# Summing the two sides of the model axis in PSUM in the first batch's cosine DFT

## The chip, the cores and the metric

The kernel runs on one core of a Trainium2 chip. The metric is the device time of one execution in microseconds, as the median of several runs. Engine names in the profile: PE is TensorE (PEld its weight loads), DVE is VectorE, ACT is ScalarE, POOL is GpSimd, SP is SyncE, whose queue issues the loads and stores here.

## What is computed

Four batches of 768 tokens, 8 heads of 64. Retention (a recurrent linear attention) comes first, then a Fourier mix over tokens and model axis, and a normalised two-layer network:

```python
for t in range(S):                                   # S = 768
    state = gamma * state + einsum('bhd,bhe->bhde', k[:, :, t], v[:, :, t])
    y[:, :, t] = scale * einsum('bhd,bhde->bhe', q[:, :, t], state)
x = y.transpose(0, 2, 1, 3).reshape(B, S, H * D)     # B = 4, H * D = 512
mixed = real(fft(fft(x, axis=1), axis=2))
u = x + mixed
un = (u - mean(u)) / sqrt(var(u) + 1e-6)
out = u + maximum(un @ w_ch1, 0) @ w_ch2             # 512 -> 2048 -> 512
```

## The kernel before

**Retention** is done in six chunks of 128 tokens, for a pair of heads at a time: transposes of q and k (tq), scores masked into atm, states by a scan (s), and the outputs wkY, which ScalarE writes as f16 into x (x0_unit in the first batch). Pair 3 is the last pair done; it fills columns 130 to 257 of side 1.

**The layout of x** serves the folds. A row of 512 channels lies as two sides: side 0 has channels 0 to 255 in order, side 1 the upper ones mirrored, so that a column holds channel d of side 0 and its mirror image of side 1. `fold_s` (L673) adds and subtracts the two halves of the token axis into xab, `fold_d` (L683) adds (e = 0, for the cosine) and subtracts (e = 1, for the sine) the two sides into eo, in two blocks of 128 columns (cb = 0, 1).

**The DFT** has two stages. Stage one, `s1_unit(b, e, cb)`, multiplies eo by tables over the token axis (csp for the cosine, ssp for the sine): six matmuls with 193 columns into one PSUM buffer, two parities of three token blocks each. A copy brings the result to g as f16, in group gi = 2e + cb. In the first batch ScalarE copies groups 0 and 1 (L737) and VectorE groups 2 and 3 (L739). Stage two, `s2_unit`, multiplies g by tables over the model axis (cd16, sd16) for one block kb of 128 tokens of the result, copies the sine part to qn (L855) and adds up u (L856, L858). `g0_unit` works out the one column that the tables leave out, and with `xmean_unit` and `mean_unit` the mean of each row, for the first three blocks of the first batch. `px_unit` adds x itself in PSUM there.

**The network.** `norm_unit` makes un, `unT_unit` transposes it (on TensorE for the first batch and for blocks 0 to 2 of the second, by DMA later), `h_unit` and `h0_unit` are the first layer, with an eviction on ScalarE for the fb in `ACT_ROWS` and on VectorE for the others, `ch_unit` the second layer, whose result is added to u and stored.

**What sets the order.** In the first batch `first_units` is a list, and `pin()` after each unit makes every engine keep the order in which the list issues instructions:

```python
    for u in first_units():
        u()
        pin()
```

`filler(n)` are n matmuls of 512 columns whose result nobody reads. From h0 on, `emit` sorts the units of all streams by due times: the products of a batch are spread evenly from b to b + 1, and the attention, the stages of the DFT and the transposes of the next batch get stretches of their own (`ts`, `da`, `dm`). A planner then sets the order of each engine by priority and readiness, starting from that order; the trace follows the due times closely but not in every place.

PSUM has a pool ps_g of five buffers for most of this, ps_y of two for wkY and px, and ps_pm of three for the network later. SyncE's loads of batch 1 wait for the last matmul of h0 for block 1 and for the weights.

Of the kernel before, what the change touches and what calls it, by code (L numbers as in the profile page):

```python
# [18 lines left out]
P = 128  # L19
# [11 lines left out]
ON_ACT = {'q': (0, 1, 0), 'kv': (1, 1, 1), 'g': (0, 1, 1), 'gr': (0, 0, 0)}  # L31
FB = 1
NPE = 2
ACT_ROWS = ((2, 4, 5, 6, 7, 8, 9, 10, 14), (0, 3, 6, 7, 9, 10, 11, 12, 14, 15), (2, 4, 5, 6, 7, 8, 9, 10, 14))


@with_exitstack
def kernel(
# [432 lines left out]
    def kv0_unit(i):  # L471
        def run():
            st = at[0, i]
            kd, v16 = kd_of[0, i], v16_of[0, i]
            wkf = st["wkf"] = ps_g.tile([P, D * (NCH - 1)], f32, tag="g", name="wkK",
                                        padded_shape=[P, DM])
            wk = wkf.rearrange("p (e c) -> p e c", c=NCH - 1)
            for c in range(NCH - 1):
                for h2 in range(2):
                    nc.tensor.matmul(wk[64 * h2:64 * h2 + 64, :, c], kd[:, c, h2, :],  # L480
                                     v16[:, c, h2, :], start=True, stop=True)
        return run
# [240 lines left out]
    def s1_unit(b, e, cb):  # L723
        def run():
            eo, g, gr = fd[b]["eo"], fd[b]["g"], fd[b]["gr"]
            tab = csp if e == 0 else ssp
            ps = ps_g.tile([P, 2, NK], f32, tag="g", name="ps1", padded_shape=[P, 2, 256])
            for par in range(2):
                for sb in range(3):
                    nc.tensor.matmul(ps[:, par, :],  # L730
                                     fd[b]["ee"][:, 2 * e + cb, par, sb, :] if b >= FB else
                                     eo[:, e, par, sb, 128 * cb:128 * cb + 128],
                                     tab[:, par, sb, :], start=(sb == 0), stop=(sb == 2))
            gi = 2 * e + cb
            dst = g[:, gi].rearrange("p (i t) -> p t i", t=2)
            if e == 0 or ON_ACT["g"][min(b, 2)]:
                nc.scalar.copy(dst, ps)  # L737
            else:
                nc.vector.tensor_copy(dst, ps)  # L739
            if b:  # L740
                (nc.scalar.copy if ON_ACT["gr"][min(b, 2)] else nc.vector.tensor_copy)(
                    gr[:, gi], g[:, gi, 384:0:-1])
        return run

    def gr_unit(gi):
# [285 lines left out]
    def first_units():  # L1031
        def a(i):
            un = [am_unit(i, 0), am_unit(i, 1)]
            return un

        def e(i, *hh):
            return [ae_unit(i, half, h2) for half, h2 in hh]

        def y(i):
            return [yi_unit(i, 0), yi_unit(i, 1)]  # L1040

        def x(i):
            return [x0_unit(i, 0), x0_unit(i, 1)]

        std = ((0, 0), (0, 1), (1, 0), (1, 1))
        heads = ((0, 0), (1, 0), (0, 1), (1, 1))
        o = PAIR_ORDER
        un = [ts_dve(0), gk_unit(o[0]), gk_unit(o[1]), t_act(0, 0), t_act(0, 1),
              q0_unit(0), t0_unit(0, 0), filler(4), ts_dve(1), te_unit(0, 0), t_act(0, 2),
              k0_unit(0), t0_unit(0, 1), filler(3), te_unit(0, 1), ts_dve(2), td_dve(0), t_act(1, 0),  # L1050
              t_act(1, 1), t_act(1, 2), v0_unit(0)]
        un += a(0) + [filler(1), kv0_unit(0)] + e(0, *std) + [sc_unit(0)]
        un += [q0_unit(1), t0_unit(1, 0), te_unit(1, 0), t_act(2, 0), t_act(2, 1), filler(4),
               k0_unit(1), t0_unit(1, 1), te_unit(1, 1)]
        un += y(0) + [parity_consts, yx_unit(0), filler(2)] + x(0) + [t_act(2, 2), v0_unit(1),
                                                                     half_ids]
        un += a(1) + [csn_unit(0), filler(1), kv0_unit(1)] + e(1, *std) + [sc_unit(1)]
        un += [q0_unit(2), t0_unit(2, 0), te_unit(2, 0), csn_unit(1), filler(3), k0_unit(2),
               t0_unit(2, 1), te_unit(2, 1)]
        un += y(1) + [td_dve(1), yx_unit(1), filler(2)] + x(1) + [  # L1060
            gk_unit(o[2]), t_act(3, 0), t_act(3, 1), v0_unit(2)]
        un += a(2) + [filler(1), kv0_unit(2)] + e(2, *std) + [sc_unit(2), t_act(3, 2),
                                                              csn_unit(2)]
        un += [q0_unit(3), w1_unit(0), t0_unit(3, 0), te_unit(3, 0), filler(3)] + y(2)
        un += [fold_s(0, 0, 258, 0, 1), g0_unit(0, (0,)), k0_unit(3), t0_unit(3, 1),
               te_unit(3, 1), yx_unit(2), gk_unit(o[3]), x0_unit(2, 0), x0_unit(2, 1),
               t_act(4, 0), t_act(4, 1), filler(2), v0_unit(3)]
        un += [w1_unit(g) for g in range(1, 4)] + [w2_unit(g) for g in range(4)]
        un += a(3) + e(3, (0, 0), (1, 0)) + [kv0_unit(3), filler(4), sc_unit(3), t_act(4, 2)]
        un += e(3, (0, 1), (1, 1))  # L1070
        un += [yx_unit(3), yi_unit(3, 0), x0_unit(3, 0), filler(1), yi_unit(3, 1), x0_unit(3, 1),
               g0_unit(0, (1,)), filler(1)]
        un += [fold_s(0, 0, 130, 1, 2), fold_d(0, 0), s1_unit(0, 0, 0), fold_s(0, 130, 258, 1, 2),
               px_unit(0), fold_d(0, 1, (0,)), xmean_unit(0), fold_d(0, 1, (1,)),
               s1_unit(0, 1, 0), s1_unit(0, 0, 1), s1_unit(0, 1, 1), g0_unit(0, (2,)),
               mean_unit(0)]
        un += [s2_unit(0, 0), px_unit(1), s2_unit(0, 1), norm_unit(0, 0), gr_unit(0), gr_unit(1),
               px_unit(2), filler(2), unT_unit(0, 0), xmean_unit(1), mean_unit(1),
               norm_unit(0, 1), s2_unit(0, 2), xmean_unit(2), mean_unit(2), norm_unit(0, 2),
               gr_unit(2), gr_unit(3), edge_zeros, x_edges(1)]  # L1080
        return un
# [25 lines left out]
    for b in range(B):  # L1107
        majors = []
        if b == 0:
            for kb in range(3):  # L1110
                if kb:
                    majors.append(unT_unit(0, kb))
                majors += [h0_unit(kb, g) for g in range(4)]
        else:
            majors += [h_unit(b, 0, fb) for fb in range(NFB)]
        majors.append(rstd_unit(b, 0))
        majors += [ch_unit(b, 0, rb3, part) for rb3 in range(3) for part in range(4)]
        majors += [h_unit(b, 1, fb) for fb in range(NFB)]
        majors.append(rstd_unit(b, 1))
        majors += [ch_unit(b, 1, rb3, part) for rb3 in range(3) for part in range(4)]  # L1120
        s2s, unTs = mix_units(b, [3, 4, 5])
        dm = (0.12, 0.24, 0.3, 0.38) if b == 0 else (0.004, 0.140, 0.232, 0.341)
        streams += [(majors, b, b + 1.0), (s2s, b + dm[0], b + dm[1]),
                    (unTs, b + dm[2], b + dm[3])]
        if b + 1 < B:
            steps = attn_steps(b + 1)
            if b == 0:
                streams.append(([load_unit(1, i, 6) for i in range(4)], 0.180, 0.220))
                streams.append(([qt_zeros], 0.1, 0.15))
                streams.append(([half_tables], 0.655, 0.655 + 0.02))  # L1130
                streams.append(([pad_unit], 0.673, 0.703))
                ts = (0.249, 0.368, 0.410, 0.415, 0.507, 0.615, 0.680, 0.685)
            else:
                streams.append(([load_unit(b + 1, i) for i in range(4)], b + -0.370, b + 0.075))
                n = [len(u) for u in steps[1:]]
                ts = [-0.040, -0.020] + [0.050 + 0.585 * sum(n[:j]) / sum(n)
                                         for j in range(6)]
            streams.append((steps[0], b + ts[0], b + ts[1]))
            streams += [(u, b + ts[j + 2], b + ts[j + 3]) for j, u in enumerate(steps[1:])]
            end = b + ts[-1]  # L1140
            da = (0.062, 0.080, 0.173, 0.203, 0.255, 0.305) if b == 0 else \
                (0.068, 0.072, 0.053, 0.163, 0.173, 0.194)
            streams.append(([s1_unit(b + 1, e, cb) for cb in range(2) for e in range(2)
                             if cb or b + 1 >= FB], end + da[0], end + da[1]))
            s2s, unTs = mix_units(b + 1, [0, 1, 2])
            streams += [(s2s, end + da[2], end + da[3]), (unTs, end + da[4], end + da[5])]
# [31 lines left out]
```

## Time and profile before

| | us |
|---|---|
| median of 8 runs (248.92 to 249.42) | 249.08 |
| the profiled execution, its own time | 249.32 |
| its span in the profile | 247.4 |
| stage one in the first batch: first fold after the last pair's scores, first copy of stage two's sine part | 27.05, 32.14 |
| first matmul of the network | 35.0 |
| granted TensorE clock | 1.00 throughout |

The profile is of one execution: 247.4 us lie between its first and last instruction, and 1.9 us around them. Starts are counted from the first instruction. The busy time of an engine says how full it was; the chain of waits follows the last instruction back to what released it, step by step.

### The profile page before, as it was taken

What the parts mean: (1) busy time and instruction counts of PE and PEld (TensorE: products, weight loads), DVE (VectorE), ACT (ScalarE), POOL (GpSimd) and SP (SyncE); (2) the same over time, 40 slices, a digit from 0 to 9 for tenths busy, and PEclk for the clock granted to TensorE, in tenths of its full rate; (3) what the DMA queues carried; (4) which work ended last, traced back from release to release, by engine and by line L of the source; (5) the groups of instructions that cost most, each with busy time, mean ns of one, the idle gap of its engine ahead of it and who ended that gap; (6) DMA issues with size and microseconds to landing.
All of it is one profiled execution on the core that took longest, in us unless ns stands there. A gap on an engine that the chain in (4) does not pass through costs nothing.

```text
span 247.4 us, 5308 instructions
## 1 busy us (share of the span) xinstructions
PE 234.6 (95%) x2024; PEld 144.3 (58%) x2024; DVE 176.0 (71%) x427; ACT 124.9 (50%) x279; POOL 81.7 (33%) x146
## 2 busy tenths in 40 slices
PE   6897899999999999999999999999999998999994
PEld 2454668956676645665567546655666455545543
DVE  8988957897788787897885748787895656424112
ACT  8798678487686434651247415642247317202500
POOL 7668500375700065791000646760002314000000
PEclk9999999999999999999999999999999999999999
DMA  8998999699999388989999468685200241221012
GB/s 177 260 256 141 201 197 202 164 236 210 302 236 214 69 170 193 194 159 133 262 268 210 98 151 200 119 138 123 84 0 3 47 145 22 45 85 42 0 45 85
DMA packets 99209, 36.39 MB, mean 147 GB/s; under 512 B 89840, under 2 KB 96240, under 8 KB 99184
## 3 DMA queue, kind: packets, MB, share of 16 engines
q1 hardware_dynamic: 94960, 31.86, 61.7%
q0 software_dynamic: 4224, 4.19, 10.4%
q8 instruction: 16, 0.26, 0.4%
q14 instruction: 9, 0.07, 0.1%
HBM read 27.26 MB, written 6.29 MB: 136 GB/s over the span
## 4 chain that ended last, share of the span: by engine, by line
PE 61%; DVE 12%; POOL 9%; DMA 6%; SPq 4%; ACT 3%; issue 3%; POOLq 0%; DVEq 0%; ACTq 0%
PE psc L973 27%; PE psh L930 19%; DMA k<-in_k_dram 5%; SPq L159 4%; PE ps L730 3%; POOL u L866 3%; DVE bst L883 3%; PE wkA L594 2%; POOL u L864 2%; PE wkY L648 2%; POOL kd L377 1%; DVE ht L936 1%; DVE u L834 1%; PE wkY L644 1%; DMA unT<-un 1%
## 5 line engine op out<-in xcount | busy, mean ns | idle before, releaser
L973 PE MATMUL psc<-w,ht 128*128 128x512 f16 (+1 forms) x400 | 89.8, 370 | 0.1
L930 PE MATMUL psh<-unT,w 128*128 128x384 f16 x448 | 81.9, 326 | 0.8 <-ACT ht L934 0.6
L973 PEld LDWEIGHTS <-ht 128*128 128x128 f16 x400 | 38.1, 98 | 35.2 <-issue 0.3
L930 PEld LDWEIGHTS <-w 128*128 128x128 f16 x448 | 42.1, 98 | 24.9 <-issue 2.1
L934 ACT ACTIVATE ht<-psh 128x384 f16<-128x384 f32 x67 | 31.7, 488 | 37.9 <-PE psh L930 37.1
L864 POOL TENSOR_TENSOR u<-u,x 128x256 f32<-128x256 f32 x21 | 13.3, 636 | 102.2 <-DVE u L834 91.8
L977 DVE SCALAR_TENSOR_TENSOR ob<-psc,stats,u 128x512 f32<-128x512 f32 (+1 forms) x25 | 18.1, 723 | 27.3 <-PE psc L973 27.2
L936 DVE TENSOR_SCALAR ht<-psh 128x384 f16<-128x384 f32 x45 | 24.7, 551 | 8.5 <-PE psh L930 7.9
L597 DVE TENSOR_TENSOR atm<-wkA,maskp 128x512 f16<-128x512 f32 x36 | 23.9, 684 | 1.1 <-PE wkA L594 1.1
L885 ACT ACTIVATE un<-u,stats 128x512 f16<-128x512 f32 x21 | 15.2, 723 | 18.5 <-DVE stats L884 14.8
L883 DVE BATCH_NORM_STATS2 bst<-u 128x6 f32<-128x512 f32 x21 | 14.6, 695 | 10.7 <-POOL u L866 10.7
L623 DVE SCALAR_TENSOR_TENSOR s<-s,gk,wkK 128x128 f16<-128x128 f16 x48 | 16.5, 343 | 2.5 <-ACT s L619 1.4
L656 ACT ACTIVATE x<-wkY,gexp 128x384 f16<-128x384 f32 x24 | 12.9, 581 | 8.3 <-PE wkY L648 8.3
L377 POOL TENSOR_SCALAR kd<-k,gexp 128x384 f16<-128x384 f32 x24 | 13.8, 587 | 3.3 <-DMA k<-in_k_dram 3.3
L145 PE MATMUL wps<-ht 128*128 128x512 f16 x40 | 12.8, 423 | 2.2 <-POOL ht L196 2.2
L866 POOL TENSOR_TENSOR u<-u,x 128x256 f32<-128x256 f32 x21 | 13.4, 637 | 3.6 <-DVE stats L884 2.4
L594 PE MATMUL wkA<-qTz,kT 128*128 128x256 f16 x72 | 13.6, 273 | 0.0
L829 ACT COPY qn<-pq 128x128 f32<-128x128 f32 x18 | 4.9, 275 | 14.6 <-PE pq L827 14.6
L947 PE MATMUL psh<-unT,w 128*128 128x128 f16 x192 | 11.5, 219 | 0.1
L947 PEld LDWEIGHTS <-w 128*128 128x128 f16 x192 | 11.0, 98 | 0.7 <-issue 0.5
L619 ACT CAST s<-wkK 128x128 f16<-128x128 f32 x12 | 3.2, 267 | 14.1 <-issue 8.6
L594 PEld LDWEIGHTS <-kT 128*128 128x128 f16 x72 | 7.0, 98 | 5.7
(164 smaller groups left out, 325.4 us busy)
## 6 DMA issues: line engine op xcount, KB each, us to landing
q<-in_q_dram SPq DMA_DIRECT2D x16, 384.0 KB, 6.4
k<-in_k_dram SPq DMA_DIRECT2D x16, 384.0 KB, 5.6
v<-in_v_dram SPq DMA_DIRECT2D x16, 384.0 KB, 6.5
out_dram<-ob SPq DMA_DIRECT2D x23, 256.0 KB, 2.6
w<-in_moe_w_ch_dram POOLq DMA_DIRECT2D x8, 512.0 KB, 11.1
out_dram<-ob SPq DMA_DIRECT2D x2, 128.0 KB, 1.7
unT<-un SPq DMA_TRANSPOSE x15, 2.4
qTz<-q16z SPq DMA_TRANSPOSE x8, 3.8
```

The lines of the kernel that those rows point to most:

```text
L594: mm = nc.tensor.matmul(wk[:, c2], st["kT"][:, c, :], st["qT"][:, :, c, :], start=True, stop=True)
L597: nc.vector.tensor_tensor(out=st["atm"][:, 2 * part:2 * part + 2], in0=wk, in1=maskp[:, PAIR_ORDER[i]].unsqueeze(1).to_broadcast([P, 2, 2, ...
L623: nc.vector.scalar_tensor_tensor(out=s16[:, c], in0=s16[:, c - 1], scalar=gk2[:, hp:hp + 1], in1=wk[:, c - c0], op0=ALU.mult, op1=ALU.add)
L864: nc.gpsimd.tensor_tensor(out=u[:, kb, 0:256], in0=u[:, kb, 0:256], in1=x[:, kb, 0, 1:257], op=ALU.add)
L866: nc.gpsimd.tensor_tensor(out=u[:, kb, 256:512], in0=u[:, kb, 256:512], in1=x[:, kb, 1, 257:1:-1], op=ALU.add)
L883: nc.vector.bn_stats(bst, u[:, kb, :])
L930: nc.tensor.matmul(psh, w116[:, cb, fb * P:(fb + 1) * P], unT[:, cb, rt * 384:(rt + 1) * 384], start=(cb == 0), stop=(cb == 3))
L934: nc.scalar.activation(ht16[:, fb, :], psh, AF.Relu, bias=0.0, scale=-1.0)
L936: nc.vector.tensor_scalar(out=ht16[:, fb, :], in0=psh, scalar1=-1.0, scalar2=0.0, op0=ALU.mult, op1=ALU.max)
L947: mm = nc.tensor.matmul(psh[:, f], w116[:, cb, fb * P:(fb + 1) * P], unT[:, cb, kb * P:(kb + 1) * P], start=(cb == 0), stop=(cb == 3))
L973: nc.tensor.matmul(psc[:, c0:c1], ht16[:, fb, rb3 * P:(rb3 + 1) * P], w216[:, fb, c0:c1], start=(fb == 0), stop=(fb == NFB - 1))
L977: nc.vector.scalar_tensor_tensor(out=ob[:, c0:c1], in0=psc[:, c0:c1], scalar=lb[b]["st"][:, rb, 3:4], in1=lb[b]["u"][:, rb, c0:c1], op0=AL ...
```

## The change

In the first batch the cosine part no longer reads eo. A new unit, `s1c_unit(cb, side)`, multiplies xab of side 0 and of side 1 by the same table, and both go into the same PSUM buffer: six matmuls for each side, twelve for a block in place of six. The six of side 0 stand early in the list, two blocks of them in place of fillers (four fillers fewer in all), and the six of side 1 after the fold that they read. `fold_d` runs for e = 1 alone. The copies are issued by a new function, `s1_evac`: for cb = 1 as two, the first with 64 of the 193 columns of each parity, which are the rows that block 0 of stage two reads.

The order in the list changes with it: VectorE's copy of group 2 stands ahead of the second fold, and `xmean_unit(0)` after the copy of group 1. Besides, fb 4 leaves ScalarE for VectorE in the first row half of batches 1 and 2, fb 9 in that of batch 3; and due times move: the transposes of un for blocks 0 to 2 of batch 1 by +0.016 of a batch, stage one, stage two and the transposes of batches 2 and 3 by -0.005.

```diff
-ACT_ROWS = ((2, 4, 5, 6, 7, 8, 9, 10, 14), (0, 3, 6, 7, 9, 10, 11, 12, 14, 15), (2, 4, 5, 6, 7, 8, 9, 10, 14))
+ACT_ROWS = ((2, 5, 6, 7, 8, 9, 10, 14), (0, 3, 6, 7, 9, 10, 11, 12, 14, 15), (2, 4, 5, 6, 7, 8, 10, 14))
...
             gi = 2 * e + cb
+            if b == 0:
+                s1_evac(gi, ps, cb == 1)
+                return
...
+    def s1_evac(gi, ps, split):
+        dst = fd[0]["g"][:, gi].rearrange("p (i t) -> p t i", t=2)
+        for i0, i1 in ((0, 64), (64, NK)) if split else ((0, NK),):
+            (nc.scalar.copy if gi < 2 else nc.vector.tensor_copy)(dst[:, :, i0:i1],
+                                                                  ps[:, :, i0:i1])
+
+    def s1c_unit(cb, side):
+        def run():
+            ab, i0 = fd[0]["ab"], 2 + 128 * cb
+            if side == 0:
+                fd[0]["ps1", cb] = ps_g.tile([P, 2, NK], f32, tag="g", name="ps1",
+                                             padded_shape=[P, 2, 256])
+            ps = fd[0]["ps1", cb]
+            for par in range(2):
+                for sb in range(3):
+                    nc.tensor.matmul(ps[:, par, :], ab[:, par, sb, side, i0:i0 + 128],
+                                     csp[:, par, sb, :], start=(side, par, sb) == (0, 0, 0),
+                                     stop=(side == 1 and sb == 2), skip_group_check=True)
+            if side == 1:
+                s1_evac(cb, ps, cb == 1)
         return run
...
-        un += a(3) + e(3, (0, 0), (1, 0)) + [kv0_unit(3), filler(4), sc_unit(3), t_act(4, 2)]
+        un += a(3) + e(3, (0, 0), (1, 0)) + [kv0_unit(3), filler(2), sc_unit(3), t_act(4, 2)]
         un += e(3, (0, 1), (1, 1))
-        un += [yx_unit(3), yi_unit(3, 0), x0_unit(3, 0), filler(1), yi_unit(3, 1), x0_unit(3, 1),
-               g0_unit(0, (1,)), filler(1)]
-        un += [fold_s(0, 0, 130, 1, 2), fold_d(0, 0), s1_unit(0, 0, 0), fold_s(0, 130, 258, 1, 2),
-               px_unit(0), fold_d(0, 1, (0,)), xmean_unit(0), fold_d(0, 1, (1,)),
-               s1_unit(0, 1, 0), s1_unit(0, 0, 1), s1_unit(0, 1, 1), g0_unit(0, (2,)),
-               mean_unit(0)]
+        un += [s1c_unit(0, 0), yx_unit(3), yi_unit(3, 0), x0_unit(3, 0), s1c_unit(1, 0),
+               yi_unit(3, 1), x0_unit(3, 1), g0_unit(0, (1,))]
+        un += [fold_s(0, 0, 130, 1, 2), s1c_unit(0, 1), fold_d(0, 0, (1,)), s1_unit(0, 1, 0),
+               fold_s(0, 130, 258, 1, 2), px_unit(0), s1c_unit(1, 1), fold_d(0, 1, (1,)),
+               xmean_unit(0), s1_unit(0, 1, 1), g0_unit(0, (2,)), mean_unit(0)]
...
-            da = (0.062, 0.080, 0.173, 0.203, 0.255, 0.305) if b == 0 else \
-                (0.068, 0.072, 0.053, 0.163, 0.173, 0.194)
+            da = (0.062, 0.080, 0.173, 0.203, 0.271, 0.321) if b == 0 else \
+                (0.063, 0.067, 0.048, 0.158, 0.168, 0.189)
```

More of the change, by code (lines that the diff above doesn't have):

```diff
@@ L742, in run @@
                     gr[:, gi], g[:, gi, 384:0:-1])
+        return run
+    def s1_evac(gi, ps, split):
[17 more added lines that the diff above has]
+                s1_evac(cb, ps, cb == 1)
         return run
```

## The prediction

> **What bounds the kernel now.** I read three views. First the page: which engine is full, and what the chain that ended last is made of.
>
> ```profile
> PE 234.6 (95%) x2024; PEld 144.3 (58%) x2024; DVE 176.0 (71%) x427; ACT 124.9 (50%) x279; POOL 81.7 (33%) x146
> PE 61%; DVE 12%; POOL 9%; DMA 6%; SPq 4%; ACT 3%; issue 3%; POOLq 0%; DVEq 0%; ACTq 0%
> ```
>
> TensorE is busy for 95% of the span, but an average hides stages. So second, busy time by stretch (stretch, its length, busy us of PE, PEld, DVE, ACT, POOL, granted clock, DMA share, GB/s):
>
> ```profile
> 27.00:35.00 8.00, 7.27 (x75) 5.02 (x71) 6.84 (x20) 4.97 (x14) 1.29 (x2) 1.00 1.23 201
> 83.00:97.00 14.00, 13.49 (x97) 7.64 (x95) 10.61 (x28) 6.80 (x17) 6.58 (x11) 1.00 0.61 133
> 97.00:113.00 16.00, 15.46 (x145) 10.06 (x144) 14.12 (x37) 9.27 (x25) 12.34 (x21) 1.00 1.00 171
> 202.00:214.00 12.00, 11.29 (x75) 6.62 (x73) 8.22 (x20) 7.21 (x19) 3.68 (x6) 1.00 0.22 56
> ```
>
> The fold and the DFT lie in 27 to 35, where VectorE is as full as TensorE. The other three rows (and 149 to 165, like 97 to 113) hold what the shifted due times and evictions can touch. Third, the chain of waits in order of time, and VectorE's own timeline beside it (start us, us, what):
>
> ```profile
> 27.14 0.55 DVE xab L673 x2
> 27.72 0.57 DVE eo L683
> 28.33 0.69 PE ps L730 x6
> 29.02 0.44 PE pq L797 x4
> 29.46 1.68 PE ps L730 x18
> 31.17 0.60 DVE g L739
> ```
>
> ```profile
> 27.72 1.03 DVE L683 TENSOR_TENSOR eo<-xab 128x768 f16<-128x768 f16 x2
> 28.66 0.62 DVE L673 TENSOR_TENSOR xab<-x 128x384 f16<-128x384 f16 x2
> 29.32 1.03 DVE L683 TENSOR_TENSOR eo<-xab 128x768 f16<-128x768 f16 x2
> 30.26 0.59 DVE L739 CAST g<-ps 128x386 f16<-128x386 f32 x1
> 31.17 0.60 DVE L739 CAST g<-ps 128x386 f16<-128x386 f32 x1 [0.32 <-PE ps L730]
> ```
>
> From 27.05 to 30.35 VectorE runs folds without a break; each fold lets six matmuls go, and the last copy of g opens stage two. After it everything hangs on the first unT through TensorE and ScalarE, so a shift here travels on: h0's last product of block 1 also releases the loads of batch 1 (SyncE waits for it until 44.78).
>
> **What the Trainium skill says.** "PSUM — Partial Sum Buffer", The four PSUM rules: two open groups in one bank cannot both carry the start flag. Both parities lie in one bank, hence the single start in s1c_unit; no operation is added for it. The same page, Engine vs sequencer instructions: VectorE's and ScalarE's queues are strict FIFO, which makes a copy placed early block the folds behind it; the trace agrees, each runs in the written order. "TensorE: Matmul & The Clock Gate", Wait — 56ns, not 53.3ns?: N / 2.4 GHz + 2.5 ns, 83 ns for 193 columns; the trace has 86 ns from start to start. "VectorE: DVE Perf Modes", Mode 1× (REGULAR): PSUM operands go one element a cycle, at 0.96 GHz.
>
> **The change part by part.** Starts below are those of single instructions in the timeline; an engine is released 0.04 to 0.06 us after the last end before it.
>
> *Taken away:* two folds into eo (e=0). Two take 1.03 us, one 0.56, so each is worth 0.48 of pace: 0.96 us of VectorE. Also four fillers (0.21 us of pace each: 0.85 us).
>
> *Added:* 12 matmuls, 12 x 0.086 = 1.03 us of TensorE. The first six (side 0, block 0) take the place of two fillers at 25.37, before yx waits for the scan until 26.28: ended at 25.9, cost nothing. Without that wait they would cost 0.5 less the fillers' 0.43. Their PSUM buffer was freed by the atm evictions (ends 24.99, 25.50, 26.67, 27.14) and the scan (26.2); five are wanted one after the other, so none waits. The next six replace one filler at 26.93: yi(3,1) starts at 27.44, not 27.14, and x0(3,1) at about 27.82, not 27.61, ending 28.39.
>
> *Moved:* VectorE's order is now fold a, one eo fold, **the copy of g 2**, fold b, one eo fold, two copies of g 3. The copy was behind all folds. Step by step:
> - Fold a ends at 27.68, the eo fold at 28.28, as before. TensorE: L773 to 27.85, s1c(0,1) 27.86 to 28.38, then s1(1,0), last end 28.38 + 5 x 0.086 + 0.25 = 29.06.
> - Copy of g 2: 29.10 to 29.69. VectorE stands idle 0.83 us, since fold b is queued behind it. Fold b 29.61 to 30.23 (was 28.66 to 29.28), eo fold to 30.82 (both cb=1 folds were done at 30.35).
> - s1c(1,1) at 30.28, last end 30.96; s1(1,1) at 30.88, last end 31.56 (was 31.13): **0.43 late**. The 0.96 saved went into the wait and the copy ahead.
> - The split copies: the whole copy is 0.59. By the page's rate 386 elements are 0.40, leaving 0.19 fixed, so 128 elements are an estimated 0.32 and 258 are 0.46. The first half ends at 31.60 + 0.32 = 31.92, against 31.77: of 0.43, 0.28 is won back. The next copy's fixed part costs 0.1 of pace, behind it. ScalarE's two for g 1 start at 31.00; the first ends near 31.3, before TensorE asks at 31.51.
> - xmean_unit(0) ran in an idle stretch of ScalarE (29.52 to 30.23). Now it stands behind g 1's second copy: 31.6 to 32.3, and the qn copy can start at 32.31, beside 32.30 from TensorE and 32.14 before. No cost of its own, but no slack either.
> - gm, g0 and mu follow g 3's second copy (32.3), so the first u starts near 32.8 instead of 32.55. It must end before the first un, which waits behind the second qn (33.02, now 33.17, and un 33.45): u ends at 33.28. Covered by 0.15; with that gone, it would delay unT by the rest.
> So unT and h0 come **0.15 us later**. The halves, which the trace doesn't show, could be 0.1 shorter or 0.2 longer: 0 to +0.4.
>
> *Evictions:* for batches 1 and 2, fb 4 of the first row half goes from ScalarE (0.49) to VectorE (0.55, pace 0.47) near 98.9, just where bst starts after 0.45 idle. u follows bst: its second part ends at 101.38, would end at 101.85, while GpSimd is busy with casts until 101.87; VectorE then has 0.87 idle. So it is hidden, or costs 0.05 each: +0.1 in two batches. For batch 3, fb 9 leaves ScalarE, but the 0.60 TensorE loses at 208.65 is the eviction of fb 8 behind un, which waits for bst behind GpSimd; that stays: 0, at best -0.6.
>
> *Due times:* sorting the units by due time before and after, batch 1's three unT units slip one product of four matmuls (0.86 us) later, and s2 of batches 2 and 3 comes one unit earlier. TensorE loses 0.58 at 91.65 and 0.26 at 93.75 to those unT. The first wait goes (un is ready at 92.39); the third unT then waits for its un (94.19, held by bst and GpSimd) with nothing left to run beside it, so h starts at 95.1 as now: 0, between -0.8 and +0.2. The s2 units move in stretches with under 0.1 us of TensorE idle: 0. No DMA is added; SyncE's transposes of unT move by a unit there, with most of a batch to spare. GpSimd gets nothing.
>
> **Sum:** +0.15 +0.1 +0 = +0.2 on the profiled execution's 249.32, which is 0.24 above the median of 249.08: **249.3** as a median.
>
> **The rivals.**
> - *Faster.* The stalls at 91.65 and 93.75 (0.84 together) and 208.65 (0.60) go, because the planner's order in those stretches becomes better with the new due times and evictions; or fold b isn't held by the copy, for which 0.9 is to be had. For: these are among the largest stalls of TensorE after 35 us. Against: un's data come at the same time. With half of it, 0.2 - 0.8 = -0.6: 248.5; with all, 247.8.
> - *Slower.* VectorE's fb 4 goes ahead of bst, and with that u, GpSimd's pass and the next bst slip; at 105.29 TensorE already loses 0.58 to u (L837). It decides from 0.46 us of delay, the slack of u ahead of GpSimd's 101.84 start. The price is up to 0.47 in each of two batches: 0.15 + 0.94 = +1.1, 250.2. For: VectorE is at 14.1 of 16 there. Against: the slack is just enough.
> - *The planner puts the later units in another order than their due times.* Either sign, some tenths; in the two cases above.
>
> **How the numbers follow.** About 0.2%, 0.5 us, is what a measurement of this kernel can tell from no change. Likeliest case, 249.3, own range 249.0 to 249.7: 0.45, of which 0.41 is within 0.2% and 0.04 slower. Faster rival 0.29. Slower rival 0.26. Together faster 0.29, same 0.41, slower 0.30. The range reaches to half of the first and to most of the second: 248.3 to 250.1.
>
> **What would show it.** Right: L683 twice in the first batch, VectorE idle about 0.8 us before its first copy of g, fold b ending near 30.2, the first h0 matmul at 35.1 to 35.2. Wrong: folds done before 30, or h0 before 34.9; a stall near 92 to 95 that shrinks by over 0.3 as a sum; the wait at 105.29 growing beyond 0.8. Then the step concerned, not the whole, is to blame.

## The result, and the profile after

The changed kernel takes 247.81 us as a median of 10 runs (247.53 to 247.89), against 249.09 for the kernel before (28 runs): a ratio of 0.9944, with a 95% interval of 0.9936 to 0.9952. That is 1.3 us faster; 249.3 was predicted, and the range ended at 248.3. The profiled execution took 247.56 us, its span is 245.7.

The page and the stretches after, with the same columns as before:

```profile
PE 234.3 (95%) x2032; PEld 145.0 (59%) x2032; DVE 176.8 (72%) x429; ACT 124.6 (51%) x277; POOL 81.4 (33%) x146
PE 71%; DVE 8%; POOL 6%; ACT 5%; SPq 3%; issue 2%; DMA 2%; POOLq 0%; DVEq 0%
```

```profile
27.00:35.00 8.00, 7.15 (x76) 5.16 (x74) 5.70 (x18) 5.18 (x16) 1.40 (x2) 1.00 1.23 203
83.00:97.00 14.00, 13.46 (x103) 8.04 (x102) 10.81 (x29) 7.33 (x20) 8.03 (x14) 1.00 0.62 135
97.00:113.00 16.00, 16.00 (x144) 10.37 (x143) 14.02 (x37) 8.94 (x20) 10.94 (x19) 1.00 0.97 167
202.00:214.00 12.00, 11.29 (x69) 6.30 (x68) 7.28 (x18) 5.91 (x15) 3.41 (x6) 1.00 0.17 35
```

In 27 to 35 VectorE has lost 1.1 us of work, and TensorE is no fuller for it. The stretch that changed is 97 to 113: TensorE was busy for 15.46 us of 16 and is now for all of them. Totals hide it: the busy time of every engine is within 1 us of before.

VectorE's timeline through the folds (in the changed kernel the copies of g are at L751):

```profile
26.82 0.62 DVE L673 TENSOR_TENSOR xab<-x 128x390 f16<-128x390 f16 x2
27.48 0.56 DVE L683 TENSOR_TENSOR eo<-xab 128x768 f16<-128x768 f16 x1
28.83 0.59 DVE L751 CAST g<-ps 128x386 f16<-128x386 f32 x1 [0.79 <-PE ps L730]
29.32 0.61 DVE L673 TENSOR_TENSOR xab<-x 128x384 f16<-128x384 f16 x2
29.96 0.56 DVE L683 TENSOR_TENSOR eo<-xab 128x768 f16<-128x768 f16 x1
31.30 0.65 DVE L751 CAST g<-ps 128x128 f16<-128x128 f32 x2 [0.78 <-PE ps L730]
```

The two eo folds for e = 0 are gone, and in their place stand two waits of 0.79 and 0.78 us for TensorE; fold b is queued behind the first. To compare profiles here, count from the last scan (L489), since everything ahead of it shifts by some tenths from one execution to the next: from its start to h0's first matmul it is 9.59 us before (25.41 to 35.00) and 9.67 after (25.18 to 34.85). The first batch is 0.08 us slower. The gain must lie later.

TensorE around batch 1's second and third transposes (pst), before:

```profile
92.44 0.40 PE L914 MATMUL pst<-ident,un 128*128 128x128 f16 x4 [0.41 <-ACT un L885]
94.90 0.34 PE L827 MATMUL pq<-gk,g16r 128*128 128x129 f16 x3
95.14 1.46 PE L930 MATMUL psh<-unT,w 128*128 128x384 f16 x8
98.73 0.40 PE L827 MATMUL pq<-gk,g16r 128*128 128x129 f16 x4
105.29 0.44 PE L644 MATMUL wkY<-s,qTz 128*128 128x64 f16 x9 [0.42 <-DVE u L837]
```

and after (L852 is stage two, L955 the first layer, L939 the transposes):

```profile
93.75 0.40 PE L939 MATMUL pst<-ident,un 128*128 128x128 f16 x4
93.98 0.40 PE L852 MATMUL pq<-gk,g16r 128*128 128x129 f16 x4
94.86 0.44 PE L613 MATMUL wkK<-v,kd 128*128 128x128 f16 x5 [0.48 <-POOL v L382]
95.13 0.40 PE L852 MATMUL pq<-gk,g16r 128*128 128x129 f16 x4
95.37 4.76 PE L955 MATMUL psh<-unT,w 128*128 128x384 f16 x28
104.38 0.46 PE L644 MATMUL wkY<-s,qTz 128*128 128x64 f16 x10
```

Stage two of blocks 3 and 4 (the x4 of pq) now stands ahead of the first layer, so block 4 comes 3.6 us earlier (0.2 us of this difference, and of the ones below, is the shift of the scan). The first layer starts at 95.37, a little later than before, but then runs through; the wait for u at 105.29 is gone. On GpSimd one sees why. Before, it waited for the u of block 3:

```profile
97.74 0.64 POOL L864 TENSOR_TENSOR u<-u,x 128x256 f32<-128x256 f32 x1 [2.65 <-DVE u L834]
```

After, it gets it 2.2 us earlier, and so do the casts of the next head pair that stand behind it in GpSimd's queue (98.94 before, 96.76 after) and the u of blocks 4 and 5 (101.84 and 104.92 before, 99.64 and 103.11 after):

```profile
95.56 0.63 POOL L889 TENSOR_TENSOR u<-u,x 128x256 f32<-128x256 f32 x1 [0.75 <-DVE u L859]
```

From there the way back to TensorE goes through VectorE's queue. The statistics of block 4 (bst) wait there for GpSimd's u, and the u of block 5, which the wkY waits for, is queued behind them. Before:

```profile
103.10 0.69 DVE L883 BATCH_NORM_STATS2 bst<-u 128x6 f32<-128x512 f32 x1 [0.87 <-POOL u L866]
104.75 0.48 DVE L837 SCALAR_TENSOR_TENSOR u<-pq,g,qn 128x256 f32<-128x256 f32 x1
```

and after:

```profile
101.29 0.69 DVE L908 BATCH_NORM_STATS2 bst<-u 128x6 f32<-128x512 f32 x1
102.93 0.49 DVE L862 SCALAR_TENSOR_TENSOR u<-pq,g,qn 128x256 f32<-128x256 f32 x1
```

Of TensorE's loss, counted as in the prediction from the starts of single matmuls against their pace, 1.09 us in 97 to 113 became 0.06; 83 to 97 stayed (0.95 and 0.91), 149 to 165 went from 1.10 to 0.85, 202 to 214 stayed (1.20 and 1.20). Together that is 1.3 us less; with the 0.08 us that the first batch loses, 1.2 of the 1.3 us measured are accounted for.

### The profile page after: what moved, and what is told of

It reads as the page before. It is cut to its first block, busy times and chain, and to the rows that moved or that the text cites. A ratio compares the mean times of both kernels' runs of the same rounds, so it can differ in the third digit from the quotient of the medians.

```text
span 245.7 us, 5325 instructions
## 1 busy us (share of the span) xinstructions
PE 234.3 (95%) x2032; PEld 145.0 (59%) x2032; DVE 176.8 (72%) x429; ACT 124.6 (51%) x277; POOL 81.4 (33%) x146
## 4 chain that ended last, share of the span: by engine, by line
PE 71%; DVE 8%; POOL 6%; ACT 5%; SPq 3%; issue 2%; DMA 2%; POOLq 0%; DVEq 0%
PE psc L998 30%; PE psh L955 23%; SPq L159 3%; PE ps L730 3%; PE psh L972 3%; PE wkA L594 3%; DMA k<-in_k_dram 2%; PE wkY L648 2%; DVE bst L908 2%; POOL u L891 2%; PE wkY L644 1%; POOL u L889 1%; PE wkK L613 1%; DVE u L859 1%; PE pq L852 1%
## 5 line engine op out<-in xcount | busy, mean ns | idle before, releaser
L955 PE MATMUL psh<-unT,w 128*128 128x384 f16 x448 | 81.3, 326 | 0.6 <-ACT ht L959 0.6
L955 PEld LDWEIGHTS <-w 128*128 128x128 f16 x448 | 42.3, 98 | 24.9 <-issue 1.3
L959 ACT ACTIVATE ht<-psh 128x384 f16<-128x384 f32 x64 | 30.7, 489 | 39.3 <-PE psh L955 38.1
L961 DVE TENSOR_SCALAR ht<-psh 128x384 f16<-128x384 f32 x48 | 26.3, 550 | 8.6 <-PE psh L955 8.3
L145 PE MATMUL wps<-ht 128*128 128x512 f16 x36 | 12.2, 450 | 2.2 <-POOL ht L196 2.2
L382 POOL TENSOR_SCALAR v<-v 128x768 f16<-128x768 f32 x12 | 10.0, 831 | 2.3 <-DMA v<-in_v_dram 2.2
```

The source lines that it names most:

```text
L955: nc.tensor.matmul(psh, w116[:, cb, fb * P:(fb + 1) * P], unT[:, cb, rt * 384:(rt + 1) * 384], start=(cb == 0), stop=(cb == 3))
L959: nc.scalar.activation(ht16[:, fb, :], psh, AF.Relu, bias=0.0, scale=-1.0)
L961: nc.vector.tensor_scalar(out=ht16[:, fb, :], in0=psh, scalar1=-1.0, scalar2=0.0, op0=ALU.mult, op1=ALU.max)
```

## The experiments

Four theories were set against each other. Theory A: the gain is made by the planner's order around batch 1's second stage. Theory B: the first batch's edit is the gain. Theory C: the moved evictions are. Theory D: the due times of all batches together are. Each kernel ran on the same chip as runs of before, and its ratio is to those.

**1. The first batch's edits alone.** The changed kernel, with `ACT_ROWS` and both `da` of before.

> The first batch's edits alone (both sides summed in PSUM, split copies, four fillers fewer), with the evictions and due times of before. Theory A (the gain is made later, by the planner's order of batch 1's second stage): 0.0 to +0.2 us against before, that is 249.1 to 249.3; h0 starts 0.1 to 0.2 us later counted from the last pair's first yx matmul; TensorE still loses about 0.6 us at the wkY near 105. Theory B (the first batch's fold is the gain): -1.0 to -1.3 us, 247.8 to 248.1, and h0 earlier by as much.

Measured: 248.91 us against 248.93, ratio 0.9998 (0.9990 to 1.0006). From the scan to h0 9.66 us, the wait at the wkY 0.57 as before; TensorE's order from h0 on is that of before. Theory B falls: what the change is named after, together with the list edits that come with it, gives nothing.

**2. All later edits, without the first batch's.**

> All later edits of the change (evictions, due times), with the first batch of before. Theory A: the same as the changed kernel within 0.2 us, so -1.1 to -1.5 against before, 247.6 to 248.0. If the two parts need each other (the planner's order depends on the first batch): less than -0.9 or more than -1.7.

Measured: 247.69 against 249.11, ratio 0.9943 (0.9931 to 0.9955), that of the whole change. The two parts don't need each other.

**3. The moved transposes alone.**

```diff
-            da = (0.062, 0.080, 0.173, 0.203, 0.255, 0.305) if b == 0 else \
+            da = (0.062, 0.080, 0.173, 0.203, 0.271, 0.321) if b == 0 else \
```

> Before, with only the due times of batch 1's first three transposes moved by +0.016. Theory A: the order of TensorE changes so that stage two of blocks 3 and 4 stands ahead of batch 1's first layer; -0.9 to -1.4 us, 247.7 to 248.2, the wait of 0.6 us at the wkY near 105 gone. Theory B: within 0.2 us of before. Theory C (evictions free the chain of batch norm statistics): within 0.2 us of before.

Measured: 248.13 against 248.93, ratio 0.9968 (0.9957 to 0.9980). TensorE's order is the new one and the wait at the wkY is gone, as theory A said, but the gain, 0.8 us, is a little under its numbers: a new wait of 0.56 us for a first-layer buffer stands ahead of the group at 107.76. In 97 to 113 TensorE loses half a microsecond less; another 0.2 us of the gain is a wait in batch 3, shown in experiment 5.

**4. The moved evictions alone.**

> Before, with only the evictions moved (fb 4 in batches 1 and 2, fb 9 in batch 3, from ScalarE to VectorE). TensorE's order is that of before. Theory A: 0 to +0.2 us. Theory C (the evictions are the gain): -0.5 to -1.3 us, with the waits at 105 and 157 shorter.

Measured: 248.00 against 248.93, ratio 0.9966 (0.9953 to 0.9978): theory A's figure was wrong and C's right. TensorE keeps its order; the wait at the wkY is 0.52, hardly shorter. What goes is another one, shown in experiment 5.

**5. Only fb 4 moved, in batches 1 and 2.**

> Before, with fb 4 alone moved from ScalarE to VectorE in batches 1 and 2 (fb 9 of batch 3 stays). If the moved evictions work through VectorE's new order at fb 12, which takes away the 0.24 us before the last first-layer group at 108 and 161: -0.5 to -0.9, about the whole of what both rows give (-0.9). If fb 9 in batch 3 carries it: within 0.3 us of before.

Measured: 248.29 against 249.11, ratio 0.9972 (0.9961 to 0.9983), not to be told apart from both rows. VectorE's timeline before, ahead of the last first-layer group of TensorE's in this stretch:

```profile
107.13 0.52 DVE L936 TENSOR_SCALAR ht<-psh 128x384 f16<-128x384 f32 x1
107.57 0.72 DVE L623 SCALAR_TENSOR_TENSOR s<-s,gk,wkK 128x128 f16<-128x128 f16 x2
108.20 0.55 DVE L936 TENSOR_SCALAR ht<-psh 128x384 f16<-128x384 f32 x1
```

and with fb 4 moved:

```profile
106.60 0.53 DVE L936 TENSOR_SCALAR ht<-psh 128x384 f16<-128x384 f32 x1
107.04 0.34 DVE L623 SCALAR_TENSOR_TENSOR s<-s,gk,wkK 128x128 f16<-128x128 f16 x1
107.30 0.55 DVE L936 TENSOR_SCALAR ht<-psh 128x384 f16<-128x384 f32 x1
```

Two evictions of ht with the state's steps between them: before two steps, now one. The second eviction frees the buffer that TensorE's last group waits for; the chain of waits before has them one after the other:

```profile
108.29 0.48 DVE ht L936
108.81 0.81 PE psh L930 x4
```

On TensorE that group starts 0.46 us after the products ahead of it before, and 0.22 after them with fb 4 moved:

```profile
108.35 0.38 PE L594 MATMUL wkA<-qTz,kT 128*128 128x256 f16 x2
108.81 0.81 PE L930 MATMUL psh<-unT,w 128*128 128x384 f16 x4
```

```profile
107.83 0.38 PE L594 MATMUL wkA<-qTz,kT 128*128 128x256 f16 x2
108.05 0.81 PE L930 MATMUL psh<-unT,w 128*128 128x384 f16 x4
```

So the loss of 0.24 us there is gone, in batch 2's turn too (161 us before): the two stages move by 0.27 and 0.26 us against before. The planner, given one more eviction on VectorE, puts VectorE's other work in another order, and that order is better. It changes ScalarE's order near there too, and no run parts the two; what TensorE waits for is VectorE's eviction.

The rest of the gain, 0.2 us, is a wait ahead of the second layer of batch 3 (its first matmul is at 212.88 before). Experiments 3 to 7 don't have it; before, the changed kernel and experiments 1, 2, 8, 9 and 10 do. With it, ScalarE's last un of batch 3 starts 0.45 us after its statistics, just as the ht eviction behind them on VectorE ends; without it 0.17 us after them. Before, and in experiment 3:

```profile
211.26 0.72 ACT L885 ACTIVATE un<-u,stats 128x512 f16<-128x512 f32 x1 [1.14 <-DVE ht L936]
```

```profile
209.90 0.72 ACT L885 ACTIVATE un<-u,stats 128x512 f16<-128x512 f32 x1 [0.85 <-DVE stats L884]
```

These two kernels have the same order on all four engines from 111 us on, so it isn't an order that decides here. Why un starts late in some kernels stays open; since the changed kernel has the wait too, it is no part of its gain.

**6. The due times of batches 2 and 3 alone.**

> Before, with only the due times of stage one, stage two and the transposes of batches 2 and 3 moved by -0.005. Theory A: within 0.2 us, at most -0.25, which is the share of the changed kernel's gain that lies at 149 to 165 us. Theory D (all gain is from due times of every batch together): -0.3 to -0.6.

Measured: 248.55 against 248.93, ratio 0.9986 (0.9980 to 0.9993): 0.35 us faster, which is in theory D's range and outside A's, though the interval (0.17 to 0.50 us) reaches into both. The losses at 105 and 157 are those of before; the one at 212 isn't there, which is 0.2 us. What else it gains isn't to be seen in the profile.

**7. Transposes and evictions moved together.**

> Moved transposes and moved evictions together, first batch and the other due times as before. If the two gains add up (0.8 and 0.9): -1.5 to -1.8 us, 247.2 to 247.5. If they take away the same waits: -1.0 to -1.2. The changed kernel itself has -1.28; theory A says that this kernel is no slower than that within 0.2 us.

Measured: 247.45 against 249.15, ratio 0.9938 (0.9926 to 0.9950). They add up. In 97 to 113 TensorE loses 0.06 us: with the evictions moved, the wait ahead of 107.76 that experiment 3 had left is gone. The due times of batches 2 and 3 add nothing to these two (experiment 2, with all three: 0.9943), which leaves little of theory D.

**8. Stage two earlier, transposes left.** Is it that TensorE no longer waits for the transposes (A2), or that u reaches GpSimd earlier (A1)?

```diff
-        dm = (0.12, 0.24, 0.3, 0.38) if b == 0 else (0.004, 0.140, 0.232, 0.341)
+        dm = (0.12, 0.24, 0.3, 0.38) if b == 0 else (-0.1, 0.14, 0.232, 0.341) if b == 1 else \
+            (0.004, 0.140, 0.232, 0.341)
```

> Before, with only the due times of batch 1's stage two for blocks 3 to 5 moved, so that TensorE has block 3 one product of four matmuls earlier and block 4 ahead of the first layer; the transposes keep their due times. Theory A1 (the gain is that u of blocks 3 and 4 gets to GpSimd earlier): -0.6 to -1.0 us, the wait of 0.58 us at the wkY near 105 gone, though the wait of 0.57 at the second transpose stays. Theory A2 (the gain is that TensorE no longer waits for the transposes): within 0.2 us.

Measured: 248.00 against 249.15, ratio 0.9959 (0.9947 to 0.9971). Its TensorE:

```profile
92.07 0.40 PE L914 MATMUL pst<-ident,un 128*128 128x128 f16 x4 [0.41 <-ACT un L885]
94.74 0.39 PE L827 MATMUL pq<-gk,g16r 128*128 128x129 f16 x4
95.42 4.71 PE L930 MATMUL psh<-unT,w 128*128 128x384 f16 x28
104.39 0.45 PE L644 MATMUL wkY<-s,qTz 128*128 128x64 f16 x10
```

The wait for the second transpose is there as before, and the whole gain of experiment 3 too: TensorE loses nothing at all in 97 to 113. GpSimd:

```profile
98.14 0.63 POOL L864 TENSOR_TENSOR u<-u,x 128x256 f32<-128x256 f32 x1 [2.19 <-DVE u L834]
99.34 0.99 POOL L374 TENSOR_SCALAR q16z<-q 128x384 f16<-128x384 f32 x2
```

The casts of the next head pair start at 99.34, no earlier than before (98.94). What is earlier is the u of block 4, 98.14 against 101.84, now ahead of the casts. So it is the time of this u that counts; the casts matter only where they stand ahead of it, as in the changed kernel.

**9. Transposes moved, stage two of blocks 4 and 5 later.** With the transposes' new due times, `dm` of batch 1 is (0.05, 0.16, 0.232, 0.341).

> The transposes of batch 1 moved by +0.016 as in the change, but stage two of blocks 4 and 5 given later due times, so that block 4 stands behind the seven first-layer groups. Theory A1: the gain of the moved transposes alone (0.8 us) is lost for the most part: 0 to -0.3 us against before, with a wait at the wkY near 105. Theory A2: -0.6 to -0.9, as with the moved transposes alone.

Measured: 248.85 against 249.15, ratio 0.9989 (0.9981 to 0.9997). With block 4 behind the first seven groups the gain is lost but for 0.3 us; the loss has moved from the wkY (0.18) to a buffer of the first layer:

```profile
108.49 0.81 PE L930 MATMUL psh<-unT,w 128*128 128x384 f16 x4 [0.43 <-DVE ht L936]
```

Experiments 8 and 9 speak for A1 and against A2.

**10. The copy of group 2 behind the folds.** In the changed kernel, every other engine keeps its order:

```diff
-        un += [fold_s(0, 0, 130, 1, 2), s1c_unit(0, 1), fold_d(0, 0, (1,)), s1_unit(0, 1, 0),
-               fold_s(0, 130, 258, 1, 2), px_unit(0), s1c_unit(1, 1), fold_d(0, 1, (1,)),
-               xmean_unit(0), s1_unit(0, 1, 1), g0_unit(0, (2,)), mean_unit(0)]
+        un += [fold_s(0, 0, 130, 1, 2), s1c_unit(0, 1), fold_d(0, 0, (1,)),
+               fold_s(0, 130, 258, 1, 2), fold_d(0, 1, (1,)), s1_unit(0, 1, 0),
+               px_unit(0), s1c_unit(1, 1), xmean_unit(0), s1_unit(0, 1, 1), g0_unit(0, (2,)),
+               mean_unit(0)]
```

> The changed kernel with VectorE's copy of group 2 moved behind both folds; every other engine keeps its order. By the prediction's step on the held fold: fold b ends near 29.0 and the second eo fold near 29.6 in place of 29.9 and 30.5, h0 0.7 to 0.9 us earlier, and the whole 0.5 to 0.9 us faster than the changed kernel: 246.9 to 247.3. If the fold's wait is covered by something else: within 0.2 us of 247.8.

Measured: 246.87 against 249.15, ratio 0.9917 (0.9901 to 0.9933), the fastest kernel of all. VectorE there:

```profile
27.78 0.56 DVE L683 TENSOR_TENSOR eo<-xab 128x768 f16<-128x768 f16 x1
28.49 0.63 DVE L673 TENSOR_TENSOR xab<-x 128x384 f16<-128x384 f16 x2 [0.15 <-ACT x L533]
29.16 0.56 DVE L683 TENSOR_TENSOR eo<-xab 128x768 f16<-128x768 f16 x1
29.63 0.59 DVE L751 CAST g<-ps 128x386 f16<-128x386 f32 x1
```

The wait of 0.79 became one of 0.15 for ScalarE's x, and from the scan to h0 it is 8.66 us: 1.01 less than in the changed kernel. From h0 to the end it takes 210.8 us, the changed kernel 210.9. So the first batch's edits together (the sum in PSUM, the split copies, fewer fillers) are worth 0.9 us against before once no copy stands ahead of the fold; which share is the sum's alone was not measured.

**11 and 12. The same for batches 2 and 3.** On top of experiment 10, `dm` of batches 2 and 3 is (-0.06, 0.04, 0.232, 0.341), then (-0.05, 0.10, 0.232, 0.341).

> The kernel with the copy behind the folds, and stage two of blocks 3 to 5 moved earlier in batches 2 and 3 too: blocks 3 and 4 stand ahead of the first layer or inside the second layer's last products. By theory A1 the 0.84 us that TensorE loses at 149 to 165 and the 0.98 at 204 to 207 go for the most part: -0.8 to -1.6 against the kernel with the copy behind the folds, 245.3 to 246.1. If in these batches the wait has another cause (ScalarE's evictions): -0.3 to +0.5.

> As the last one, but only block 3 of stage two stands ahead of the first layer in batches 2 and 3, block 4 two groups later. By theory A1 a smaller gain: -0.4 to -1.0 against the kernel with the copy behind the folds. If the wait has another cause: -0.3 to +0.5.

Measured: 248.52, ratio 0.9990 (0.9976 to 1.0004), and 248.26, ratio 0.9968 (0.9955 to 0.9981), against 249.11. Both are slower than experiment 10, by 1.8 and 1.3 us by the ratios; A1's figures for these batches were wrong. In the first of them TensorE now waits earlier, for VectorE:

```profile
147.71 0.81 PE L955 MATMUL psh<-unT,w 128*128 128x384 f16 x4 [0.25 <-DVE ob L1002]
150.65 0.81 PE L955 MATMUL psh<-unT,w 128*128 128x384 f16 x4 [0.17 <-DVE ht L961]
```

It lost 0.84 in 149 to 165 and now loses 0.66 there and 0.69 ahead of it, at the first layer's buffers, and 1.1 us at 200 to 202 in batch 3. That VectorE's u and statistics, drawn forward, hold up the evictions is what the releasers suggest, but wasn't tried by itself. The second one's profile has a wait of 1 us for a transpose by DMA ahead of the matmul at 112.92 and is of a run far above its median (249.30 us); I read nothing from it.

## Why the prediction was wrong, step by step

- **The first batch: right.** +0.15 us was worked out and 0.08 found, from the scan to h0. The held fold (0.83 us of idle VectorE predicted, 0.79 measured), the copies (0.32 and 0.46 estimated for VectorE, 0.31 and 0.44 measured), TensorE's pieces at no cost: all as said. Only the first u was mis-sized: counted from the scan it starts 0.08 us later, not 0.25. The 0.9 us named for a fold that isn't held was right as well (experiment 10: 1.01 less to h0 than in the changed kernel).
- **Due times: the step that failed first.** "With nothing left to run beside it" was the error. I had the units' due times but took the planner to follow them there, and forgot that stage two of blocks 3 and 4 was ready. The first layer starts no earlier, as said, and the loss in 83 to 97 stays; but what was pulled in there is what GpSimd waited for. The sum put this term at 0, and left the 0.58 us at 105.29 standing. I priced the stretch by its own stalls and did not follow what the pulled-in units feed ten microseconds on: GpSimd's u of block 4, VectorE's statistics behind it, the u of block 5, the wkY. Moved transposes alone gain 0.8 us (experiment 3), of which 0.5 lie there and 0.2 are the open wait in batch 3.
- **Evictions: the second.** I inserted 0.47 us into VectorE's queue as it stood, and got +0.1. The planner gave VectorE a new order, and fb 4 alone gains 0.7 us (experiment 5): 0.5 in two waits of 0.24 us, at 108.81 and 161.63, which the prediction does not list, and 0.2 in the open wait. The slack that I worked out, 0.46 us, was never the point.
- **The other due times:** 0 predicted; alone 0.35 faster (experiment 6), on top of the other two nothing. 0.2 of it is the open wait, the rest has no known cause.
- **fb 9:** no effect predicted; with it 0.9966, without it 0.9972, not to be told apart.
- **The rivals.** The faster one named the planner's order, which was right, but the wrong stalls: those at 93.75 and 208.65 are still there (0.23, with 0.64 for GpSimd's v at 94.86 beside it, and 0.60). The slower one's wait at 105.29 is just the one that went away. In the last paragraph, L683 twice and VectorE's idle time were found as forecast, and h0 too when counted from the scan (35.08 on the clock of before; 34.85 as the profile has it). The stalls at 92 to 95 sum to 0.87, as before (0.84). So none of these signs told of the miss: the wait at 105.29 was watched for growth only.

The mistake in kind: the largest chance, 0.41 against 0.29 for faster, was put on "no change" because the edit with a visible cost was small, while two edits that look like mere numbers go through a planner and have no price that can be read from a row.

## What to carry to other kernels

Price an edit by which instruction it puts ahead of which in a queue, not by the work it saves: the same edits of the first batch gave nothing with a copy ahead of the next fold and 0.9 us without. When a due time or an engine of one eviction changes under a planner, build the order of every engine and compare it before any arithmetic, and follow what each moved unit feeds, through GpSimd and VectorE here, to the wait at the far end. An order that helps one batch needn't help the next, as the last two experiments show.

## What was not expected of the hardware

The parts before the last scan shift by up to 0.5 us between executions (the scan starts at 24.96 to 25.48 us in the profiles of fourteen kernels that do the same up to there but for two fillers), so stages are to be compared from a mark inside them. A split of a copy from PSUM costs less than feared (0.1 us more was estimated, 0.06 found): 386 columns took 0.59 us on VectorE, the two parts of 128 and 258 columns 0.65 together, first start to last end; on ScalarE 0.60 and 0.62.
